# Wide attention tiles: scores shifted and keys summed on the vector engine, one exponential per tile, and the plan that goes with it

## The chip, the core and the metric

The kernel runs on one core of a Trainium2 chip. The metric is the device time of one execution in microseconds (us), median over the runs. Five engines of the core take part: TensorE (PE in the profile, with its weight loads as PEld), VectorE (DVE), ScalarE (ACT), GpSimd (POOL), and SyncE (SP), which issues the DMAs. Each engine works through its own queue in order, and waits on semaphores for the others.

## What is computed

Attention over 4 batches of 8 heads, 576 positions, 64 values per head, is the sum of two parts, one over positions pooled by four and one over a band of seven keys. Its output is the input of two feed-forward layers.

```python
q_d = q.reshape(B, H, Sd, factor, D).mean(axis=3)      # k_d, v_d the same
out_up = np.repeat(sm_attn(q_d, k_d, v_d), factor, axis=2)
mask = np.abs(pos[:, None] - pos[None, :]) < factor
scores = np.where(mask, scale * np.matmul(q, k.transpose(0, 1, 3, 2)), -1e9)
attn = np.exp(scores - np.max(scores, axis=-1, keepdims=True))
attn = attn / (np.sum(attn, axis=-1, keepdims=True) + 1e-09)
x = out_up + np.matmul(attn, v)                        # 2304 tokens x 512
...
xn = x / rms * rms_g
h1 = (silu(xn @ w_gate) * (xn @ w_val)) @ w_out        # 512 -> 1536 -> 512
out = (np.maximum(h1 @ w_in, 0.0) ** 2) @ w_out2       # 512 -> 2048 -> 512
```

## The kernel before

**The two layers.** Every large matrix product is done as three products of float32r parts (high x high, high x low, low x high), so each weight half and each activation exists as a high and a low tile (`xh` and `xl` for the normalised tokens, `hh` and `hl` for the hidden values). The first layer works on nine blocks of 256 tokens (`BLK`) and six slices of 256 hidden columns. A step is `hidden(j, fp)` (lines 920 to 937: 24 matmuls into bank `g`, 24 into bank `v`, then tanh, two multiplications and the split into `hh` and `hl`) and, one step later, `outp(j, fp)` (24 matmuls into the banks `a` or `b`). The string `SEQ` gives the blocks of the first twelve steps, `011100001101`: block 0 once, block 1 three times, and so on. The second layer follows with blocks of 512 tokens.

**The weights** come in as float64 words, and `decode` (line 543) turns each half of 512 columns into float32 high and low parts: a DMA, two passes on ACT, three to four on DVE, an integer addition and a subtraction that POOL or DVE may take (`VP`). For two of the weight tiles, `TAGS` sends an intermediate to a PSUM bank (`a3`, `g1`), and then some of this is done on DVE alone.

**The attention of batch 0** (blocks 0, 1 and a quarter of block 2) is done by PE: `down(b, pr)` (line 614) is the pooled part for a pair of heads, `wide(t)` (line 702) the banded part for 96 tokens and all eight heads, t = 0 to 5, and `wide_post(t)` (line 737) multiplies by v, adds the pooled part, normalises, transposes and writes the columns of `xh` and `xl`. In `wide`, PE writes the scores of four head pairs side by side into two banks (96 tokens by 4 x 104 keys each). DVE takes the maxima (two reductions of 96x416) and scales them; ACT takes eight exponentials of 96x104, each with its own bias and with an accumulator output that gives the sum over keys. Then PE transposes the eight results. The batches 1 to 3 are done without PE, by `local` (line 799) on POOL and DVE, and `post` (line 856).

**What sets the order.** Nothing is issued in program order. The calls are recorded in the order of the string `PLAN` (a = wide, b = wide_post, d = down, w = weights, u = local units, p = post, x = a step of the first layer), and `Plan.order` (line 365) then places every operation on its engine by its own table of costs, going forth and back `ROUNDS` times with some random jitter `JIT`; operations with a choice of engines go to the one that finishes first. `Plan.trace` (line 434) issues them in that order. Where PE would idle before the first block's matmuls, `trace` puts in filler matmuls on the identity (line 466) that write bank `v` and are used by nobody:

```python
fill = fill and not op.ends        # ends: another matmul writes slot v0
if fill and free:
    for _ in range(int((s - free) * FILL / 0.22)):
        self.nc.tensor.matmul(out=out, lhsT=one, rhs=one, start=True, stop=True)
```

All operations are issued from one line (473 before, 472 after the change; fillers 466 and 465), so the profile is read by tile names. `b` followed by a number in the order of instructions is a slice of one of sixteen big SBUF tiles or a PSUM bank `b`; the profile leaves the number out.

Of the kernel before, what the change touches and what calls it, by code (L numbers as in the profile page):

```python
# [48 lines left out]
TAGS = ('dbg- dtg- dbg- dgg- bdd- bdd- bdd- bdd- ttd- ttd- ttd- ttd- add- add- add- add- '  # L49
        'aagg aagg aagt bbtd bbdd bbtd bdt tdt gta gdt gdt btt '  # L50
        '-- -- a3 a3 -- -- -- -- -- -- -- -- -- -- -- -- -- -- -- g1 g1 -- -- -- -- -- -- -- -- -- -- -- -- -- -- --')
SEQ = '011100001101'
PLAN = 'd2 d3 d0 d1 a0 b0 w00 a2 a1 w01 w12 b1 a4 b2 a3 a5 w11 w21 b4 w20 w10 b3 w02 w30 u1 w32 b5 d7 u0 d5 d4 d6 w22 E w31 w41 w40 w50 x x w42 x x d10 x x w52 w51 x x x x x p2 x u2 d11 u3 p3 x d8 x x u5 d9 u4 x x x p4 u6 x x d12 x x x d15 d14 d13 x u7 p5 u8 x u9 x x x x x p6 x x x u10 x x x u11 x x p7 x x u12 u13 x x x x x x x x p8 x x x x x x'
SLOT = [7, 8, 9, 1, 0, 4, 5, 2, 6, 3, 0, 1, 3, 4, 5, 2]
ROUNDS = 38
# [7 lines left out]
JIT = 0.3  # L63
# [413 lines left out]
def attn_moe_kernel(ctx: ExitStack, tc, qs, kw, vw, qt, kt, vt, v4, wg, wv, wo, w2i, w2o, gw, gb,  # L477
# [6 lines left out]
    seq1 = [(int(c), SEQ[:i].count(c)) for i, c in enumerate(SEQ)]  # L484
    seq1 += [(j, fp) for j in range(len(set(SEQ)), len(BLK)) for fp in range(NP1)]
# [57 lines left out]
    def decode(src, n, hi, lo, st, how="--"):  # L543
# [6 lines left out]
        low = lw if how[0] == "-" else bank(how[0], I32)  # L550
        A.activation(low, lw.bitcast(U32), AF.Copy, scale=2.0**-29)
        part = lw if how[1] == "1" else low
        V.scalar_tensor_tensor(out=part, in0=hw, scalar=-0x40000000, in1=low, op0=ALU.bitwise_and,
                               op1=ALU.bitwise_or)
# [5 lines left out]
        if how[1] in "-1":  # L560
            VP.tensor_tensor(out=hw, in0=hw, in1=part, op=ALU.add)
        else:
            V.tensor_tensor(out=low if how[1] == "3" else hw, in0=hw, in1=low, op=ALU.add)
        if how[1] == "3":
            hf = low.bitcast(F32)
        AV.copy(hi[:, cs], hf)
        (V if how[1] == "3" else VP).tensor_tensor(out=lo[:, cs], in0=hf, in1=hi[:, cs].bitcast(F32), op=ALU.subtract)
# [27 lines left out]
    def weights1(fp, m):  # L595
        src = (wg, wv, wo)[m]
        n = fp * 3 + m
        how = TAGS.split()[28 + 2 * n:30 + 2 * n]
        hi, lo = slots(n) if n < 16 else [spare([128, 1024], F32R) for i in range(2)]
        for n in range(2):  # L600
            st = staging() if fp < 5 else tile("stage", "st", [128, 512, 2], I32, 3)
            decode(src[fp], n, hi, lo, st, how[n])
        W1[fp, m] = hi, lo
# [8 lines left out]
    wq, wk, wod = [None] * 4, [None] * 4, [None] * 4  # L612

    def down(b, pr):
# [24 lines left out]
        V.tensor_reduce(out=qs, in_=q[:, 0:S].rearrange("p (s f) -> p s f", f=FAC), axis=AX.X, op=ALU.add)  # L639
# [5 lines left out]
        kf = k[:, 4:4 + S].rearrange("p (s f) -> p f s", f=FAC)  # L645
        if tags[3] == "-":
            V.tensor_reduce(out=ks, in_=k[:, 4:4 + S].rearrange("p (s f) -> p s f", f=FAC), axis=AX.X, op=ALU.add)
        P.memset(vs[:, :, :, 64:65], 4.0)
        V.tensor_reduce(out=vs.rearrange("p c h e -> p (c h) e")[:, :, 0:64], in_=v4s, axis=AX.X, op=ALU.add)
        sps = bank(tags[0])[0:96, 0:432].rearrange("p (c t) -> p c t", c=3)  # L650
        with plan.joint():
            for c in range(3):
                for f in range(1 if tags[3] == "-" else FAC):
                    T.matmul(out=sps[:, c, :], lhsT=qbd[:, c].rearrange("p h t -> p (h t)"),
                             rhs=ks if tags[3] == "-" else kf[:, f], start=(c == 0 and f == 0), stop=(c == 2),
                             skip_group_check=True)
# [45 lines left out]
    def wide(t):  # L702
# [476 lines left out]
```

## Time and profile before

| what | value |
|---|---|
| median of 3 runs | 1001.02 us (1000.61 to 1002.26) |
| the profiled execution: time | 1000.25 us |
| its span (first to last instruction) | 998.0 us |
| PE busy | 980.2 us, 6866 instructions |
| DVE busy | 587.6 us, 985 instructions |
| ACT busy | 417.0 us, 984 instructions |
| POOL busy | 442.3 us, 298 instructions |
| mean granted PE clock | 0.998 |

A float32 matmul appears in the trace as two instructions (two passes). Durations of instructions that follow each other on an engine overlap by some tens of ns, so a start-to-start distance is a little shorter than a duration. Filler matmuls count as busy time of PE.

### The profile page before, as it was taken

How to read it: one execution, taken by the hardware profiler on the slowest of the kernel's cores; microseconds unless marked ns; L12 is line 12 of the kernel's file. 1: busy time of each engine (PE TensorE's matmuls, PEld its weight loads, DVE VectorE, ACT ScalarE, POOL GpSimd, SP SyncE). 2: the span in 40 equal slices, each digit the busy share in tenths (PEclk: the TensorE clock that was granted, in tenths of full speed). 3: DMA queues.
4: the chain of work that ended last, by engine and by line, in shares of the span. 5: the costliest groups of instructions: out<-in, count | busy, mean ns of one | idle time of the engine just before them, and what ended most of it. 6: DMA issues, size and time to landing. Idle time of an engine off the chain costs nothing.

```text
span 998.0 us, 17246 instructions
## 1 busy us (share of the span) xinstructions
PE 980.2 (98%) x6866; PEld 906.4 (91%) x6866; DVE 587.6 (59%) x985; ACT 417.0 (42%) x984; POOL 442.3 (44%) x298
## 2 busy tenths in 40 slices
PE   7998999999999999999999999999999999999998
PEld 7888999999999999999999998888888888888897
DVE  6999899786687857575634568963222322322232
ACT  5787665532435342323244557663222212322232
POOL 2566688867656676676733465863001000100000
PEclk9999999999999999999999999999999999999999
DMA  9954553253262523222011446334000100100010
GB/s 282 262 160 157 175 179 103 73 151 113 85 182 80 171 78 115 93 65 96 28 33 60 132 128 209 104 109 137 1 1 1 54 0 1 43 1 1 1 43 22
DMA packets 38465, 92.93 MB, mean 93 GB/s; under 512 B 4218, under 2 KB 14498, under 8 KB 38386
## 3 DMA queue, kind: packets, MB, share of 16 engines
q1 hardware_dynamic: 38386, 91.84, 29.6%
q8 instruction: 54, 0.88, 0.4%
q14 instruction: 25, 0.20, 0.1%
HBM read 80.62 MB, written 11.21 MB: 92 GB/s over the span
## 4 chain that ended last, share of the span: by engine, by line
PE 89%; DVE 5%; POOL 2%; DMA 2%; issue 1%; ACT 1%; SPq 0%; DVEq 0%; POOLq 0%; ACTq 0%
PE v L473 25%; PE g L473 24%; PE a L473 20%; PE b L473 15%; DVE b L473 2%; PE d L473 2%; DVE st L473 2%; PE t L473 2%; PE v L466 1%; DMA b<-in_qt 1%; DMA st<-in_wg 1%; POOL w L473 0%; POOL st L473 0%; POOL pr L473 0%; POOL b L473 0%
## 5 line engine op out<-in xcount | busy, mean ns | idle before, releaser
L473 PE MATMUL g<-xh,w 128*128 128x256 f32 (+1 forms) x776 | 176.8, 307 | 0.4 <-DVE th L473 0.4
L473 PE MATMUL v<-xh,w 128*128 128x256 f32 (+1 forms) x632 | 147.6, 311 | 0.5 <-DVE hl L473 0.5
L473 DVE SCALAR_TENSOR_TENSOR v<-v,th 128x512 f32<-128x512 f32 (+1 forms) x94 | 63.3, 674 | 128.6 <-ACT th L473 101.3
L473 PEld LDWEIGHTS g<-xh,w 128*128 128x128 f32 x776 | 131.1, 191 | 7.0 <-ACT xh L473 0.6
L473 ACT ACTIVATE th<-g 128x512 f32<-128x512 f32 (+1 forms) x94 | 54.5, 580 | 198.1 <-PE g L473 194.8
L473 POOL TENSOR_TENSOR pr<-v,es 128x896 f32<-128x896 f32 x54 | 99.4, 1939 | 65.7 <-DVE es L473 28.2
L473 PE MATMUL v<-xh,b 128*128 128x256 f32 (+1 forms) x552 | 123.9, 303 | 0.1
L473 POOL TENSOR_TENSOR pr<-k,q 128x896 f32<-128x896 f32 x54 | 115.4, 2158 | 9.6 <-DVE sc L473 7.2
L473 PE MATMUL g<-xl,w 128*128 128x256 f32 (+1 forms) x388 | 118.3, 305 | 0.1
L473 PEld LDWEIGHTS v<-xh,w 128*128 128x128 f32 x632 | 107.7, 191 | 7.1 <-PE g L473 0.7
L473 POOL TENSOR_TENSOR xl<-st,xh 128x1024 fp32r<-128x1024 f32 (+1 forms) x10 | 21.6, 2179 | 184.7 <-ACT xh L473 184.7
L473 PE MATMUL v<-xl,w 128*128 128x256 f32 (+1 forms) x316 | 97.9, 310 | 0.0
L473 PEld LDWEIGHTS v<-xh,b 128*128 128x128 f32 x552 | 93.0, 191 | 4.4 <-PE g L473 0.3
L473 PE MATMUL g<-xh,b 128*128 128x256 f32 (+1 forms) x408 | 94.4, 310 | 0.2 <-DVE th L473 0.2
L473 ACT CAST hh<-v 128x512 fp32r<-128x512 f32 (+1 forms) x94 | 53.5, 569 | 81.6 <-DVE v L473 71.3
L473 PE MATMUL v<-xl,b 128*128 128x256 f32 (+1 forms) x276 | 83.1, 301 | 0.0
L473 DVE SCALAR_TENSOR_TENSOR g<-g,th 128x512 f32<-128x512 f32 (+1 forms) x40 | 25.8, 645 | 95.5 <-ACT th L473 95.4
L473 DVE TENSOR_TENSOR hl<-v,hh 128x512 fp32r<-128x512 f32 (+1 forms) x94 | 62.4, 664 | 26.3 <-ACT hh L473 24.6
L473 PEld LDWEIGHTS g<-xl,w 128*128 128x128 f32 x388 | 74.1, 191 | 3.6 <-DVE xl L473 0.3
L473 POOL TENSOR_TENSOR st<-st 128x512 int32<-128x512 int32 x48 | 55.9, 1166 | 41.5 <-DVE st L473 39.4
L473 PEld LDWEIGHTS g<-xh,b 128*128 128x128 f32 x408 | 69.1, 190 | 4.2 <-issue 0.3
L473 ACT ACTIVATE st<-st 128x512 int32<-128x512 uint32 (+1 forms) x96 | 64.7, 684 | 18.7 <-DVE st L473 11.2
(207 smaller groups left out, 2336.8 us busy)
## 6 DMA issues: line engine op xcount, KB each, us to landing
k<-in_kw SPq DMA_DIRECT2D x12, 640.0 KB
v<-in_vw SPq DMA_DIRECT2D x12, 640.0 KB
st<-in_w2i SPq DMA_DIRECT2D x14, 512.0 KB
st<-in_w2o SPq DMA_DIRECT2D x14, 512.0 KB
y<-vv SPq DMA_DIRECT2D x18, 256.0 KB
out<-xh SPq DMA_DIRECT2D x18, 256.0 KB
st<-y SPq DMA_DIRECT2D x8, 512.0 KB
st<-in_wg SPq DMA_DIRECT2D x7, 512.0 KB
```

What stands on the lines that cost most here:

```text
L466: self.nc.tensor.matmul(out=out, lhsT=one, rhs=one, start=True, stop=True)
L473: getattr(self.hw[on[op]], method)(*args, **kw)
```

## The change

In `wide`, with a fifth letter in the tile's entry of `TAGS` (all six tiles have one now), DVE adds the negated maxima to the scores and writes the shifted scores to SBUF (two instructions of 96x416), ACT takes one exponential over all 96x832 in place, and DVE sums it over the keys (one reduction of 832 to 8). The scaling of the maxima and the eight exponentials with their accumulators go. In `down`, a sixth, fifth or fourth letter sends the pooling sum of v, q or k to PE (`total`, four matmuls with the identity that add up in a bank, and a copy by ACT or DVE); it is used for v of pair 0 and k of pair 3 of batch 0. In `decode` the variants through PSUM go. `PLAN`, `SLOT`, the banks in `TAGS`, `ROUNDS` (38 to 5) and `JIT` (0.3 to 0.05) are others, so the whole order is another; `SEQ` is kept, as the last word of `TAGS`.

```diff
-TAGS = ('dbg- dtg- dbg- dgg- bdd- ...
-        'aagg aagg aagt bbtd bbdd bbtd bdt tdt gta gdt gdt btt '
+TAGS = ('dbg--b dtg--- dbg--- dggt-- bdd--- ...
+        'aaggm aaggm aagtm bbtdm bbddm bbtdm bdt tdt gtd gdt vdt btt '
+        '011100001101')
...
+    def total(parts, tag):
+        n = math.prod(parts.index.shape[1:])
+        p = parts.parts[1] - parts.parts[0]
+        o = bank(tag)[0:p, 0:n]
+        with plan.joint():
+            for f in range(FAC):
+                T.matmul(out=o, lhsT=id_sb[0:p, 0:p], rhs=parts[:, f], start=f == 0, stop=f == FAC - 1)
+        return o
...
+        elif tags[3] != "p":
+            AV.copy(ks, total(kf, tags[3]))
...
+            AV.copy(vo, total(v4s.rearrange("p g d f -> p f g d"), tags[5]).rearrange("p (g d) -> p g d", g=4))
...
         for h in range(2):
             V.tensor_reduce(out=nm[:, 4 * h:4 * h + 4], in_=sp[h], axis=AX.X, op=ALU.max, negate=True)
-        V.tensor_scalar(out=nm, in0=nm, scalar1=SCALE, scalar2=None, op0=ALU.mult)
-        for h in range(2):
-            for r in range(4):
-                i = 4 * h + r
-                A.activation(p[:, h, r], sp[h][:, r], AF.Exp, bias=nm[:, i:i + 1], scale=SCALE,
-                             accum_out=sm_[:, i:i + 1])
+            for h in range(2):
+                V.tensor_tensor(out=p[:, h], in0=sp[h], in1=nm[:, 4 * h:4 * h + 4].unsqueeze(2).to_broadcast([WT, 4, WK]),
+                                op=ALU.add)
+            pf = p.rearrange("p h r k -> p (h r) k")
+            A.activation(pf, pf, AF.Exp, scale=SCALE)
+            V.tensor_reduce(out=sm_, in_=pf, axis=AX.X, op=ALU.add)
```

The places of the order on which the prediction rests follow, first those before, then those of the change.

DVE's queue at the first wide tile. `b_89` is a slice that holds maxima and sums, `a` the bank of the scores, `b_244` the exponentials of the tile. Before:

```order
L473 TENSOR_REDUCE b_89<-a 96x4 x2
L473 TENSOR_SCALAR b_89<-b_89 96x8
L473 TENSOR_SCALAR rc<-g 72x4
L473 TENSOR_REDUCE vs<-w_203 72x4x64
L473 RECIPROCAL rc<-rc 72x4
L473 TENSOR_REDUCE nm<-d 96x3
```

After:

```order
L472 TENSOR_REDUCE b_89<-a 96x4 x2
L472 TENSOR_TENSOR b_244<-a,b_89 96x416 x2
L472 SCALAR_TENSOR_TENSOR st<-st 128x512
L472 TENSOR_SCALAR rc<-g 72x4
L472 TENSOR_REDUCE vs<-w_190 72x4x64
L472 RECIPROCAL rc<-rc 72x4
L472 TENSOR_REDUCE nm<-d 96x3
L472 TENSOR_TENSOR b_313<-g,rc 72x256
L472 TENSOR_REDUCE b_89<-b_244 96x8
```

The scaling is gone from behind the maxima; two additions stand there, and a sum over 832 elements stands six instructions further down. The same holds for all six tiles.

PE's queue ahead of the first matmul of block 0 (`v_1104`, after the change `v_791`). `v_134` are fillers, `t` and `d` are transposes and the pooled part in banks. Before:

```order
L473 MATMUL b_995<-b8_412,b6_200 96x64 x8
L466 MATMUL v_134<-id_101 128x128 x19
L473 MATMUL t_1059<-id_101,b9_470 128x96 x4
L473 MATMUL d_1067<-id_101,pe_1025 72x96 x3
L466 MATMUL v_134<-id_101 128x128 x3
L473 MATMUL b_1078<-b11_351,qbd_95 96x144 x3
...
L473 MATMUL v_1104<-xh_554,w16_796 128x256
```

After:

```order
L472 MATMUL v_721<-b8_349,b5_417 96x64 x8
L472 MATMUL d_753<-id_101,b9_502 128x96 x4
L472 MATMUL t_759<-id_101,b3_675 104x96 x4
L472 MATMUL t_776<-id_101,b1_461 104x96 x4
L472 MATMUL d_783<-id_101,b3_675 104x96 x4
L472 MATMUL v_791<-xh_563,w18_639 128x256
```

One wide_post now multiplies into bank `v` (`v_721`), which ends the fillers; before, they run up to the last matmuls ahead of block 0. In all there are 151 filler matmuls before and 64 after.

PE's queue at the first matmul of block 1 (`g_1239`, after the change `g_1119`; `xh_1010` and `xh_770` are block 1). Before:

```order
L473 MATMUL g_1176<-xh_554,w15_429 128x256
L473 MATMUL t_1213<-id_101,b9_470 128x96 x4
L473 MATMUL d_1229<-id_101,pe_1169 72x96 x3
L473 MATMUL g_1239<-xh_1010,w14_408 128x256
```

After:

```order
L472 MATMUL d_1085<-id_101,pe_1067 72x96 x3
L472 MATMUL t_1095<-id_101,b9_502 128x96 x4
L472 MATMUL d_1108<-id_101,pe_1067 72x96 x3
L472 MATMUL g_1119<-xh_770,w14_362 128x256
```

In both, the transposes of the last wide tile (`t_1213`, `t_1095`) stand right ahead of it, and 48 matmuls of 128x256, all of block 0, are ahead of that. Before, the second half of them comes directly in front; after the change they are all done earlier, with small matmuls in between.

DVE's queue at the last columns of block 1 (`xl_1018`, after the change `xl_774`). Before:

```order
L473 SCALAR_TENSOR_TENSOR b9_470<-t_1093,b15_89,b7_337 96x512
L473 SCALAR_TENSOR_TENSOR b12_442<-b12_442 128x512
L473 RECIPROCAL rc_1173<-rc_1173 72x4
L473 TENSOR_SCALAR b13_262<-b13_262 128x512
L473 TENSOR_TENSOR pt_1224<-d_1122,rc_1173 72x256
L473 SCALAR_TENSOR_TENSOR th_1220<-th_1220,g_1176 128x512
L473 TENSOR_TENSOR xl_1018<-t_1213,xh_1010 128x4x32
```

After:

```order
L472 SCALAR_TENSOR_TENSOR b9_502<-t_999,b15_89,b7_269 96x512
L472 TENSOR_TENSOR es_1059<-es_1059,ssum_1069 128x2x2x7
L472 TENSOR_REDUCE vs_1032<-b14_442 72x4x64
L472 TENSOR_SCALAR b13_227<-b13_227 128x512
L472 SCALAR_TENSOR_TENSOR th_958<-th_958,g_888 128x512
L472 TENSOR_TENSOR xl_774<-t_1095,xh_770 128x4x32
```

Ahead of this point DVE has, of decode, 20 bitwise combinations (SCALAR_TENSOR_TENSOR of `st` or `b`) and 35 TENSOR_SCALAR before, 19 and 38 after; four more decode instructions that read bank `a` only before; and of the local attention four reductions of 896 elements before (two `sc<-pr`, two `xa<-pr`), two after (`sc<-pr`).

## Rows read from the trace of the kernel before

**Rows 1.** The page: span, and busy time (share, instructions) of each engine.

```profile
span 998.0 us, 17246 instructions
...
PE 980.2 (98%) x6866; PEld 906.4 (91%) x6866; DVE 587.6 (59%) x985; ACT 417.0 (42%) x984; POOL 442.3 (44%) x298
```

**Rows 2.** Busy time of each engine by stretches; the first column is the stretch.

```profile
core 0: us, PE busy (x) PEld busy (x) DVE busy (x) ACT busy (x) POOL busy (x), PEclk, DMA share, GB/s
3.79:104.73 100.94, 92.68 (x841) 84.77 (x842) 89.92 (x171) 75.28 (x229) 55.23 (x47) 0.98 0.70 215
104.73:205.00 100.27, 98.90 (x843) 98.18 (x844) 89.33 (x133) 56.38 (x119) 77.95 (x55) 1.00 0.45 135
205.00:990.00 785.00, 784.58 (x5167) 720.42 (x5166) 405.85 (x675) 282.86 (x634) 308.82 (x191) 1.00 0.23 72
```

**Rows 3.** Timeline of PE: start, duration, what, and idle time before it.

```profile
71.11 0.90 PE L473 MATMUL b<-b,qbd 128*96 128x144 f32 x6
...
72.29 1.04 PE L473 MATMUL d<-b,b 72*96 72x128 f32 x8
...
91.94 1.54 PE L473 MATMUL b<-b,qbd 128*96 128x144 f32 x6 [1.15 <-ACT st L473]
...
93.75 1.91 PE L473 MATMUL t<-b,b 72*96 72x128 f32 x8
...
104.73 0.35 PE L473 MATMUL g<-xh,w 128*128 128x256 f32 x1 [0.44 <-DVE th L473]
```

**Rows 4.** Timeline of DVE: a tile's maxima and scaling, the last maxima, block 1's last columns.

```profile
17.09 1.07 DVE L473 TENSOR_REDUCE b<-a 96x4 f32<-96x416 f32 x2
18.20 0.17 DVE L473 TENSOR_SCALAR b<-b 96x8 f32<-96x8 f32 x1
...
65.05 0.57 DVE L473 TENSOR_REDUCE b<-b 96x4 f32<-96x416 f32 x1
...
104.88 0.29 DVE L473 TENSOR_TENSOR xl<-t,xh 128x128 fp32r<-128x128 f32 x1 [0.29 <-ACT xr L473]
```

**Rows 5.** Groups of DVE by form, 0 to 150 us: busy us, mean ns, idle before.

```profile
L473 DVE TENSOR_REDUCE w<-w 128x144 f32<-128x576 f32 x8 | 5.9, 744 | 3.8 <-DMA w<-in_qt 3.7
...
L473 DVE TENSOR_REDUCE vs<-w 72x256 f32<-72x1024 f32 x4 | 4.8, 1209 | 0.0
...
L473 DVE TENSOR_REDUCE sc<-pr 128x14 f32<-128x896 f32 x4 | 4.3, 1069 | 0.0
...
L473 DVE TENSOR_TENSOR b<-g,b 96x512 f32<-96x512 f32 x3 | 2.0, 680 | 0.0
...
L473 DVE CUSTOM_DVE_ANT_0 a<-st,a 128x1024 uint16<-128x1024 uint16 x1 | 0.7, 680 | 0.0
```

**Rows 6.** ACT: groups of a tile's exponentials, a longer activation by form (0 to 110 us).

```profile
L473 ACT ACTIVATE b<-a,b 96x104 f32<-96x104 f32 x24 | 8.0, 344 | 1.8 <-DVE b L473 1.8
...
L473 ACT ACTIVATE b<-b 128x512 f32<-128x512 f32 x9 | 6.2, 692 | 0.7 <-DVE b L473 0.7
...
L473 ACT ACTIVATION_READ_ACCUMULATOR b<-a,b 96x1 f32 x24 | 4.9, 203 | 0.0
```

**Rows 7.** Timeline of ACT: the sixth tile's last exponential.

```profile
79.82 0.34 ACT L473 ACTIVATE b<-b,b 96x104 f32<-96x104 f32 x1
```

**Rows 8.** Waits of DVE, 3.7 to 105.2 us: total, times, longest.

```profile
DVE b L473 <- POOL b L473: 2.7, 2, 1.4
...
DVE b L473 <- ACT b L473: 1.1, 1, 1.1
```

**Rows 9.** Groups of POOL by form, 0 to 200 us: a decode's addition and its subtraction.

```profile
L473 POOL TENSOR_TENSOR st<-st 128x512 int32<-128x512 int32 x20 | 22.9, 1145 | 10.7 <-DVE st L473 10.4 <-DVE b L473 0.4
...
L473 POOL TENSOR_TENSOR w<-b,w 128x512 fp32r<-128x512 f32 x9 | 12.9, 1437 | 4.7 <-ACT w L473 4.7
```

**Rows 10.** Groups of PE by form, 0 to 150 us: the fillers.

```profile
L466 PE MATMUL v<-id 128*128 128x128 f32 x302 | 40.9, 285 | 0.0
```

More of the change, by code (lines that the diff above doesn't have):

```diff
@@ L62 @@
 FILL = 0.8
-JIT = 0.3
+JIT = 0.05
 SEED = 1
@@ L483, in attn_moe_kernel @@
     blk2 = [(n, min(512, NT - n)) for n in range(0, NT, 512)]
-    seq1 = [(int(c), SEQ[:i].count(c)) for i, c in enumerate(SEQ)]
-    seq1 += [(j, fp) for j in range(len(set(SEQ)), len(BLK)) for fp in range(NP1)]
+    seq = TAGS.split()[-1]
+    seq1 = [(int(c), seq[:i].count(c)) for i, c in enumerate(seq)]
+    seq1 += [(j, fp) for j in range(len(set(seq)), len(BLK)) for fp in range(NP1)]
     seq2 = [(j, f) for j in range(len(blk2)) for f in range(2 * NP2)]
@@ L541, in attn_moe_kernel, with decode @@
     late = []
-    def decode(src, n, hi, lo, st, how="--"):
+    def decode(src, n, hi, lo, st):
         DQ.dma_start(out=st.rearrange("p n w -> p (n w)"),
@@ L549, in decode @@
         hf = hw.bitcast(F32)
[L550 to L554, printed above, removed]
+        A.activation(lw, lw.bitcast(U32), AF.Copy, scale=2.0**-29)
+        V.scalar_tensor_tensor(out=lw, in0=hw, scalar=-0x40000000, in1=lw, op0=ALU.bitwise_and, op1=ALU.bitwise_or)
         plan.either(A=lambda e: e.activation(hf, hf, AF.Abs),
@@ L559, in decode @@
                         op1=ALU.logical_shift_left)
[L560 to L565, printed above, removed]
+        VP.tensor_tensor(out=hw, in0=hw, in1=lw, op=ALU.add)
         AV.copy(hi[:, cs], hf)
-        (V if how[1] == "3" else VP).tensor_tensor(out=lo[:, cs], in0=hf, in1=hi[:, cs].bitcast(F32), op=ALU.subtract)
+        VP.tensor_tensor(out=lo[:, cs], in0=hf, in1=hi[:, cs].bitcast(F32), op=ALU.subtract)
     stages = [0, 0]
@@ L597, in weights1 @@
         n = fp * 3 + m
-        how = TAGS.split()[28 + 2 * n:30 + 2 * n]
         hi, lo = slots(n) if n < 16 else [spare([128, 1024], F32R) for i in range(2)]
@@ L601, in weights1 @@
             st = staging() if fp < 5 else tile("stage", "st", [128, 512, 2], I32, 3)
-            decode(src[fp], n, hi, lo, st, how[n])
+            decode(src[fp], n, hi, lo, st)
         W1[fp, m] = hi, lo
@@ L638, in down @@
         pt = tile("dn", "pt", [72, 2, 2, 3, 48])
-        V.tensor_reduce(out=qs, in_=q[:, 0:S].rearrange("p (s f) -> p s f", f=FAC), axis=AX.X, op=ALU.add)
+        qf = q[:, 0:S].rearrange("p (s f) -> p f s", f=FAC)
+        kf = k[:, 4:4 + S].rearrange("p (s f) -> p f s", f=FAC)
+        if tags[4] == "-":
+            V.tensor_reduce(out=qs, in_=qf.rearrange("p f s -> p s f"), axis=AX.X, op=ALU.add)
+        else:
+            qs = total(qf, tags[4])
         for h in range(2):
@@ L652, in down @@
             for c in range(3):
-                for f in range(1 if tags[3] == "-" else FAC):
+                for f in range(FAC if tags[3] == "p" else 1):
                     T.matmul(out=sps[:, c, :], lhsT=qbd[:, c].rearrange("p h t -> p (h t)"),
-                             rhs=ks if tags[3] == "-" else kf[:, f], start=(c == 0 and f == 0), stop=(c == 2),
+                             rhs=kf[:, f] if tags[3] == "p" else ks, start=(c == 0 and f == 0), stop=(c == 2),
                              skip_group_check=True)
@@ L720, in wide @@
             V.tensor_reduce(out=nm[:, 4 * h:4 * h + 4], in_=sp[h], axis=AX.X, op=ALU.max, negate=True)
-        V.tensor_scalar(out=nm, in0=nm, scalar1=SCALE, scalar2=None, op0=ALU.mult)
-        for h in range(2):
-            for r in range(4):
-                i = 4 * h + r
-                A.activation(p[:, h, r], sp[h][:, r], AF.Exp, bias=nm[:, i:i + 1], scale=SCALE,
-                             accum_out=sm_[:, i:i + 1])
+        if tags[4] == "-":
+            V.tensor_scalar(out=nm, in0=nm, scalar1=SCALE, scalar2=None, op0=ALU.mult)
+            for h in range(2):
+                for r in range(4):
+                    i = 4 * h + r
+                    A.activation(p[:, h, r], sp[h][:, r], AF.Exp, bias=nm[:, i:i + 1], scale=SCALE,
+                                 accum_out=sm_[:, i:i + 1])
+        else:
+            for h in range(2):
+                V.tensor_tensor(out=p[:, h], in0=sp[h], in1=nm[:, 4 * h:4 * h + 4].unsqueeze(2).to_broadcast([WT, 4, WK]),
[3 more added lines that the diff above has]
+            V.tensor_reduce(out=sm_, in_=pf, axis=AX.X, op=ALU.add)
         V.tensor_scalar(out=sm_, in0=sm_, scalar1=1e-9, scalar2=None, op0=ALU.add)
```

18 lines of the change are left out of this document (9 added, 9 removed).

## The prediction

> **What bounds the kernel now.** I read the page first, for who is busy. PE is, with 98% of the span, DVE with 59% [rows 1]. A share over the whole span hides that the program has two regimes, so the second view is the busy time by stretches [rows 2]. From 205 to 990 us PE is busy 784.58 of 785.00 us: the feed-forward layers run without a gap, and nothing beside PE counts. From 104.73 to 205 us it is busy 98.90 of 100.27 us. Before 104.73 us DVE is busy 89.92 of 100.94 us, ACT 75.28 and POOL 55.23. PE shows 92.68 us there too, but much of that is filler: 302 passes of 285 ns, which overlap [rows 10], are used by nobody.
>
> What ends the first regime is in the timeline of PE: at 104.73 us the first matmul of block 1 starts [rows 3], and from then on the PE is full. It can start when the last columns of block 1 are written, which DVE does at 104.88 us, some 0.15 us behind the first pass, for the low part [rows 4]. I call this point **the gate**. Behind it PE has the same work in both versions: counting the order up to the gate, the forms and numbers of PE's instructions agree but for the fillers, the eight matmuls of the pooling sums that the change adds ahead of it, and three small ones each way. So the time moves by what the gate moves, plus any new stall behind it. The fillers themselves are no gain: they fill time in which PE waits anyway.
>
> **The sum.** DVE's queue up to the gate holds all six wide tiles in both versions, so I price what the change puts into and takes out of it.
>
> - Added: twelve additions of 96x416 from PSUM. The trace has no such form; the nearest row multiplies a bank of 96x512 by a broadcast factor in 680 ns [rows 5], so 680 x 416/512 = 553 ns, in all 6.6 us. Six sums of 96x832: a reduction of 896 elements takes 1069 ns [rows 5], so 993 ns, in all 6.0 us. Together 12.6 us. Bounds: start to start some 0.08 us less each, so 11.2, and up to 13 if a longer tile costs a little more.
> - Removed: six scalings at 0.17 us [rows 4], 1.0 us; the pooling sums of k and v for one pair each, 744 and 1209 ns [rows 5], 1.95 us; four decode instructions through bank a, each like the one of 680 ns [rows 5], 2.7 us. Two reductions of 896 elements for the local attention stand behind the gate now, 2.1 us. The rest of decode is as much as before (one combination less, three scalar passes more), taken at nothing, give or take 0.5 us.
>
> That is 12.6 - 1.0 - 1.95 - 2.7 - 2.1 = **+4.9 us** of DVE work ahead of the gate.
>
> DVE was idle for 100.94 - 89.92 = 11.0 us there [rows 2]. More work in an in-order queue covers some waits. DVE waited 2.7 us for POOL's powers and 1.1 us for ACT [rows 8]; ACT has less to do now. Eight exponentials at 344 ns and eight accumulator reads at 203 ns [rows 6] go for one instruction of 832 elements, by the row of 692 ns for 512 elements about 1.1 us. I let half of these 3.8 us go: **-2.0 us**, between 0 and the whole 11.0.
>
> The clock. The granted clock is 0.98 over the first stretch [rows 2], with one low place: at 91.94 us, behind an idle time of 1.15 us, six passes take 1.54 us that took 0.90 at 71.11, and at 93.75 eight take 1.91 where a like group took 1.04 at 72.29 [rows 3]. That place cost 0.6 + 0.9 = 1.5 us, at the lower of the two levels (1.2 GHz). The change leaves 64 of 151 fillers and ends them far ahead of the gate, when one product is written into bank v; between the first 48 matmuls of block 0 and the gate PE has only small work. I expect block 1 to begin at the low level and lose this once: **+1.5 us**, between 0 and 3. The Trainium skill says the same of idle gaps (TensorE: Matmul & The Clock Gate, Why this matters for your kernels): matmul bursts are to follow each other without gaps, or the array falls back to its lower clock. The one low place of the trace agrees with it.
>
> Taken at nothing: the eight added pooling matmuls and their copies (in the first 15 us, where PE and ACT wait for DMAs and DVE); the two decode halves whose addition and subtraction go from DVE to POOL, 2 x (1145 + 1437) = 5.2 us [rows 9], since POOL is busy 55.23 of 100.94 us [rows 2]; and the two reductions put off, since DVE is idle 100.27 - 89.33 = 10.9 us from 104.73 to 205 [rows 2]. If that cover is gone, the second rival holds. Wide scores also leave their banks earlier, when DVE has added and not when ACT has finished; this only helps PE, which waits.
>
> 4.9 - 2.0 + 1.5 = +4.4 us on the profiled execution's 1000.25 us (span 998.0), 1004.7 us. The median of the runs is 0.77 us above that execution, so **1005.4 us**.
>
> A rule of the skill stands against this reading. By Perfetto Trace Analysis, Identifying the Most-Contended Engine, the engine with the highest occupancy is the one to optimize; over the span that is PE, and by it 12.6 us on an engine at 59% [rows 1] would cost nothing, some 1001 us. The stretches [rows 2] contradict it for the first 105 us; the same page, under Optimization Strategy, grants that the most contended engine may change between regimes.
>
> **The rivals.**
>
> *Faster: the chain of the tiles, not DVE's queue, sets the gate.* The sixth tile's maxima end at 65.6 us [rows 4], but its last exponential comes at 79.82 us [rows 7], since ACT takes the eight one by one between other work. In the change, two additions (1.1 us) and one exponential (1.1 us) follow the maxima, so the tile could be ready some 12 us sooner. But DVE has to get through its queue: with no idle time at all it needs 89.9 + 4.9 = 94.8 us where the stretch took 100.9, so the gate comes at most 6.1 us sooner, 995 us; halfway 998 us. It decides for "faster" if DVE's idle time ahead of the gate falls from 11.0 us to under 4. For it: the idle time is all waits for others, and the whole order is another. Against it: DVE's queue is mostly work of decode and down, placed between the tiles.
>
> *Slower still: what is put off does not fit behind the gate.* The two reductions (2.1 us) and POOL's 5.2 us come due before block 2 is needed at about 205 us; POOL is busy 77.95 and DVE 89.33 of 100.27 us there [rows 2]. If none of it fits, 1005.4 + 7.3 = 1012.7 us. It decides once PE idles by several us between the gate and the end of block 1's steps, where it idled 1.4 us.
>
> *No change.* DVE's waits take up the 4.9 us whole and the clock stays high at the gate, 1001 us.
>
> That the change does not do what it says is excluded: all six tiles have the fifth letter, and the order shows twelve additions of 96x416 and six exponentials of 96x832. Only the maxima were on DVE already, so that part changes nothing.
>
> **How the numbers follow.** No change is within 0.2%, 999 to 1003 us; less than this a measurement can't tell. The forecast (gate late by 2 to 9 us, 1003 to 1009) has 0.44, slower still 0.13, no change 0.15, faster 0.28: the order is wholly rearranged, and a few us of waits decide. So slower by over 0.2% has 0.57. The range leaves under one in ten on each side: from the lower bound of the faster rival, 995, to the second rival's time, 1012.5.
>
> **What would show it.** Right: the first matmul of block 1 starts 2 to 7 us after 104.73 us; DVE is busy over 90% of the time until then, with twelve additions near 0.55 us and six sums near 1.0 us; the clock reads below 1.00 in the stretch before it, and behind it PE idles as little as before. The step on the waits is wrong if DVE's idle time up to the gate is under 6 us; the step on the clock, if block 1's first passes run at full pace. The whole is wrong if the gate comes before 103 us, or if PE is fuller ahead of it with block 0's or other useful steps than the order lets me see.

## The result, and the profile after

The changed kernel takes 1012.33 us (median of 4 runs, 1011.6 to 1013.95), the kernel before, beside it on the same chip, 1001.64 us (4 runs, 1000.61 to 1005.26): ratio 1.0102, 95% interval [1.0073, 1.0132]. The change makes it slower by 10.7 us; forecast were 4.4. The profiled execution took 1013.95 us, its span is 1011.9 us.

The page, which answers to [rows 1]: PE is busy for about as long as before, DVE 6.8 us longer, ACT 11.5 us less.

```profile
span 1011.9 us, 16829 instructions
...
PE 982.2 (97%) x6708; PEld 904.1 (89%) x6708; DVE 594.4 (59%) x991; ACT 405.5 (40%) x896; POOL 445.9 (44%) x302
```

Busy time by stretches, which answers to [rows 2]. The stretch up to the gate is shown whole and in three pieces.

```profile
core 0: us, PE busy (x) PEld busy (x) DVE busy (x) ACT busy (x) POOL busy (x), PEclk, DMA share, GB/s
3.79:25.00 21.21, 19.61 (x132) 16.25 (x133) 11.26 (x21) 8.58 (x26) 0.20 (x2) 1.00 0.99 289
25.00:75.00 50.00, 41.51 (x387) 34.84 (x385) 48.97 (x90) 30.62 (x59) 27.89 (x23) 0.92 0.55 166
75.00:115.71 40.71, 29.70 (x167) 26.97 (x165) 32.76 (x69) 26.87 (x58) 28.18 (x24) 0.58 0.49 151
3.79:115.71 111.92, 90.82 (x681) 78.06 (x681) 92.99 (x178) 66.07 (x142) 56.28 (x49) 0.81 0.61 184
115.71:205.00 89.29, 89.29 (x734) 89.29 (x735) 80.05 (x116) 48.88 (x100) 70.07 (x49) 0.95 0.44 141
```

The same pieces of the kernel before:

```profile
3.79:25.00 21.21, 19.52 (x174) 18.40 (x175) 16.34 (x28) 11.46 (x41) 4.84 (x5) 1.00 0.98 305
25.00:75.00 50.00, 47.86 (x456) 41.95 (x455) 46.73 (x96) 40.55 (x134) 30.60 (x24) 1.00 0.71 211
75.00:104.73 29.73, 25.30 (x217) 24.42 (x216) 26.86 (x49) 23.27 (x56) 19.79 (x19) 0.94 0.48 158
```

The gate, block 1's first matmul, has moved from 104.73 to 115.71 us, by 11.0 us. DVE's work ahead of it has grown by 92.99 - 89.92 = 3.1 us, its idle time from 11.02 to 18.93 us, by 7.9. By pieces (length less DVE busy) that idle time was 4.87, 3.27 and 2.87 us before and is 9.95, 1.03 and 7.95 us now: between 25 and 75 us DVE hardly pauses any more, and 5.1 us came in on either side.

The timeline of PE shows what stands in the first piece, a late group of the tiles, and the gate, which answers to [rows 3]:

```profile
5.26 1.73 PE L472 MATMUL d<-w,b 128*96 128x144 f32 x6 [5.26 <-DVE w L472]
7.12 3.84 PE L472 MATMUL b<-w,id 72*72 72x256 f32 x8
10.79 2.23 PE L472 MATMUL t<-w,id 128*128 128x144 f32 x8
...
14.68 1.50 PE L472 MATMUL d<-w,qbd 128*96 128x144 f32 x6
...
17.99 0.90 PE L472 MATMUL d<-w,b 128*96 128x144 f32 x6
...
81.46 1.97 PE L472 MATMUL d<-b,b 72*96 72x128 f32 x8
...
115.71 0.55 PE L472 MATMUL g<-xh,w 128*128 128x256 f32 x1 [0.97 <-ACT pt L472]
...
124.80 0.55 PE L472 MATMUL v<-xh,w 128*128 128x256 f32 x2
125.18 0.28 PE L472 MATMUL v<-xl,w 128*128 128x256 f32 x1
```

The second and third rows are the pooling sums that the change moved to PE. They take from 7.12 to 12.84 us and stand ahead of the scores of the next pair of heads (14.68). PE is at half pace here: the group at 5.26 takes 1.73 us, the same form at 17.99 takes 0.90, although the clock column reads 1.00 for this piece. The kernel before starts at half pace too, but 18 fillers stand where the pooling sums stand now, and full pace is there by 11.05 us:

```profile
5.49 1.72 PE L473 MATMUL d<-w,b 128*96 128x144 f32 x6 [5.49 <-DVE w L473]
7.00 3.71 PE L466 MATMUL v<-id 128*128 128x128 f32 x18
...
11.05 0.90 PE L473 MATMUL d<-w,qbd 128*96 128x144 f32 x6
```

Behind the gate the first pass takes 0.55 us where it took 0.35 [rows 3]; only at 125.2 us are passes back to 0.28.

The timeline of DVE, which answers to [rows 4]: the two longest waits, and block 1's last columns.

```profile
16.21 0.60 DVE L472 TENSOR_REDUCE nm<-d 96x3 f32<-96x432 f32 x1 [4.99 <-PE d L472]
...
83.53 0.69 DVE L472 TENSOR_TENSOR d<-b,d 96x512 f32<-96x512 f32 x1 [3.75 <-PE d L472]
...
115.49 0.28 DVE L472 TENSOR_TENSOR xl<-t,xh 128x128 fp32r<-128x128 f32 x1
```

Both waits are for PE: the first for the scores behind the pooling sums, the second for the group at 81.46, which stands behind block 0's passes at half pace and takes 1.97 us where a like group took 1.04 [rows 3]. The forms of DVE up to the gate (busy us, mean ns, idle before), which answer to [rows 5]:

```profile
L472 DVE TENSOR_REDUCE b<-b 96x8 f32<-96x832 f32 x6 | 6.0, 1005 | 0.0
...
L472 DVE TENSOR_TENSOR b<-a,b 96x416 f32<-96x416 f32 x6 | 3.2, 576 | 0.0
L472 DVE TENSOR_TENSOR b<-b,b 96x416 f32<-96x416 f32 x6 | 3.2, 573 | 0.0
```

### The profile page after: what moved, and what is told of

It reads as the page before. It is cut to its first block, busy times and chain, and to the rows that moved or that the text cites. A ratio compares the mean times of both kernels' runs of the same rounds, so it can differ in the third digit from the quotient of the medians.

```text
span 1011.9 us, 16829 instructions
## 1 busy us (share of the span) xinstructions
PE 982.2 (97%) x6708; PEld 904.1 (89%) x6708; DVE 594.4 (59%) x991; ACT 405.5 (40%) x896; POOL 445.9 (44%) x302
## 4 chain that ended last, share of the span: by engine, by line
PE 90%; DVE 5%; POOL 2%; issue 2%; DMA 1%; ACT 1%; SPq 0%; POOLq 0%
PE g L472 25%; PE v L472 25%; PE a L472 20%; PE b L472 16%; DVE b L472 3%; PE d L472 2%; PE t L472 2%; POOL w L472 1%; POOL b L472 1%; DVE st L472 1%; DVE xl L472 0%; DMA w<-in_v 0%; ACT xh L472 0%; POOL st L472 0%; DMA od<-pt 0%
## 5 line engine op out<-in xcount | busy, mean ns | idle before, releaser
L472 PE MATMUL g<-xh,w 128*128 128x256 f32 (+1 forms) x776 | 180.4, 311 | 1.0 <-ACT pt L472 1.0
L472 PE MATMUL v<-xh,w 128*128 128x256 f32 (+1 forms) x632 | 150.8, 316 | 0.0
L472 PEld LDWEIGHTS g<-xh,w 128*128 128x128 f32 x776 | 134.1, 195 | 7.7 <-ACT pt L472 1.3
L472 PEld LDWEIGHTS v<-xh,w 128*128 128x128 f32 x632 | 110.0, 195 | 6.4
```

Of the source, the lines that this page charges most:

```text
L472: getattr(self.hw[on[op]], method)(*args, **kw)
```

## The experiments

Twelve kernels, each beside runs of the kernel before on its own chip. All keep the order of the kernel they start from: the plan is made as there, and in `trace` an operation's calls are replaced at its place (`swap`, an empty list for none), or fillers are added or left out. So a difference comes from the edit and from the waits that it shifts, not from a new plan. The table sums them up: the gate in the profile, what the span is beyond it, DVE's busy and idle time from 3.79 us to the gate, and the ratio of the runs to before.

| kernel | gate | span - gate | DVE busy | DVE idle | ratio [95%] |
|---|---|---|---|---|---|
| before | 104.73 | 893.3 | 89.92 | 11.02 | 1 |
| after | 115.71 | 896.2 | 92.99 | 18.93 | 1.0102 [1.0073, 1.0132] |
| e1 before, fillers end early | 109.98 | 894.3 | 89.76 | 16.43 | 1.0028 [1.0010, 1.0046] |
| e2 after, fillers up to the gate | 121.03 | 892.8 | 98.01 | 19.23 | 1.0119 [1.0086, 1.0152] |
| e3 before, maxima three times | 114.18 | 894.7 | 102.91 | 7.48 | 1.0084 [1.0057, 1.0111] |
| e4 after, short sums | 112.77 | 895.6 | 88.69 | 20.29 | 1.0054 [1.0038, 1.0070] |
| f5 after, pooling sums on DVE | 113.44 | 893.8 | 96.68 | 12.97 | 1.0056 [1.0029, 1.0083] |
| f6 after, old exponentials | 117.99 | 895.9 | 83.74 | 30.46 | 1.0165 [1.0135, 1.0194] |
| f7 before, wide part | 118.56 | 895.1 | 102.08 | 12.69 | 1.0106 [1.0073, 1.0138] |
| f8 after, f5 and f6 together | 119.11 | 893.9 | 86.74 | 28.58 | 1.0130 [1.0107, 1.0152] |
| g1 before, wide part, sums earlier | 115.84 | 894.0 | 101.21 | 10.84 | 1.0112 [1.0065, 1.0158] |
| g2 after, fillers in unused columns | 128.53 | 893.8 | 96.40 | 28.34 | 1.0200 [1.0159, 1.0240] |
| g3 before, two decodes on POOL | 114.11 | 894.9 | 86.97 | 23.35 | 1.0048 [1.0028, 1.0069] |
| h1 f5 with fillers in a free bank | 112.74 | 893.8 | 96.56 | 12.39 | 1.0065 [1.0051, 1.0079] |

The third column holds within 3.4 us over all fourteen, while the gate ranges over 24 us: whatever is edited ahead of the gate, the rest of the kernel follows it as it is. The profiles are single executions and scatter by some us against the medians, so the ratios decide where the two disagree (as for e1 and g3). A difference between two of the kernels carries both intervals, some 3 to 4 us.

**Is it the clock? (e1, e2)** e1 ends the fillers of the kernel before at 60 us of the plan, as the change does:

```diff
-                    if fill and free:
+                    if fill and free and s < 60.0:
```

> The kernel before in its own order, but with no fillers placed after 60 us of the plan, where the changed kernel places its last ones. Theory A (the loss of the changed kernel is the clock: without fillers PE falls to the low level ahead of the gate, its small matmuls of the tile chain take twice as long, and block 1 starts at half pace): the granted clock falls to about 0.5 to 0.7 between 65 and 105 us, the gate moves from 104.7 to 109 or later, and the time is 5 to 10 us longer, 1006 to 1011. Theory B (the loss is DVE's longer queue, the clock costs little): the gate stays within 2 us and the time within 3 us, 1001 to 1004.

Measured: 1.0028, 2.8 us. DVE's work is the same, but it idles 5.4 us more, and the gate comes at 109.98 us, at full pace. The low clock of the stretch ahead (0.82 against 0.98 in that stretch) delays what DVE waits for; the runs put that at 2.8 us, about a quarter of the change's loss.

e2 gives the changed kernel 93 more fillers from 65 us to the gate, each in the bank that the next group of matmuls writes:

```diff
+    for _ in range(more):      # 93 in all, ahead of 12 groups
+        self.nc.tensor.matmul(out=fb[:, 0:128], lhsT=one, rhs=one, start=True, stop=True)
```

> The changed kernel in its own order, with 93 more fillers between 65 us and the first matmul of block 1, each written into the bank that the next group of matmuls overwrites. Theory A: the clock stays at 1.0 up to the gate, the gate moves from 115.7 to 107 to 110, block 1 starts at full pace, and the time falls by 6 to 9 us, to 1003 to 1006. Theory B: the gate stays after 112, only the low stretch behind it goes, and the time falls by 2 to 4 us, to 1008 to 1010.

Measured: 1.0119, not better than the change. Block 1 begins at full pace and the span beyond the gate falls to 892.8 us, but the gate comes at 121.03. The wait of 3.75 us for PE is gone; two other things took its place. A filler that writes the next group's bank waits until that bank is free, and then stands in front of the group, as PE's timeline shows (line 472 is the filler):

```profile
73.66 3.35 PE L472 MATMUL t<-id 128*128 128x128 f32 x14 [2.70 <-ACT b L479]
...
88.73 4.77 PE L472 MATMUL g<-id 128*128 128x128 f32 x26 [3.07 <-DVE b L479]
```

And DVE's idle time is only 0.3 us more than after the change, but the same 178 instructions keep it busy 5.0 us longer. Part of it is three TENSOR_SCALAR that took 0.99 us after the change and take 2.96 here, while POOL runs two subtractions (84.79 to 87.70 us; the last section comes back to this). First the change, then e2:

```profile
84.47 0.99 DVE L472 TENSOR_SCALAR b<-b 128x512 f32<-128x512 f32 x3
85.04 2.96 DVE L479 TENSOR_SCALAR b<-b 128x512 f32<-128x512 f32 x3
```

The gain behind the gate, 896.2 - 892.8 = 3.4 us, is about what the low level costs there; the gate's place is not explained by the clock.

**Is it DVE's queue? (e3, e4)** e3 issues each of the twelve maxima of the kernel before three times, e4 cuts the change's six sums from 104 keys per head to one:

```diff
+    if on[op] == "V" and calls[0][2].get("negate") and calls[0][2]["out"].shape == (96, 4):
+        calls = calls * 3
...
+    if method == "tensor_reduce" and kw["out"].shape == (96, 8):
+        kw = dict(kw, in_=kw["in_"][:, :, 0:1])
```

> The kernel before in its own order, each of the twelve maxima issued three times: 24 x 0.53 = 12.7 us of added DVE work, as much as the additions and sums of the change, nothing taken away, fillers as they are. Theory B: the gate moves by 8 to 13 us and the time is 1009 to 1014. Theory A: DVE's waits take up a good part, the gate moves by at most 5 us, 1002 to 1006.

> The changed kernel in its own order, the six sums over 832 elements cut to one key per head (the denominators are left out but for one term): 6 x 0.9 = 5.4 us less DVE work ahead of the gate. Theory B: the gate moves from 115.7 to 110 to 111 and the time falls by 4 to 6 us, to 1006 to 1008. Theory A: PE's and ACT's waits stay, and the time falls by less than 2 us, 1010 to 1013.

Measured: e3 has 13.0 us more DVE work, 3.5 us less idle time, the gate 9.45 us later and ratio 1.0084; e4 4.3 us less work, the gate 2.9 us earlier and ratio 1.0054, 4.8 us below the change. So work on DVE moves the gate, at some 0.7 us per us, in both orders. The maxima and the sums also stand in the chain of their own tile, so these two runs do not tell DVE's queue from that chain.

**The parts of the change undone (f5, f6, f8).** f5 makes the two pooling sums with one DVE reduction each again:

```diff
             AV.copy(ks, total(kf, tags[3]))
+            plan.ops[-2].swap = []
+            plan.ops[-1].swap = [("V", "tensor_reduce", (), dict(out=ks, in_=kf..., axis=AX.X, op=ALU.add))]
```

> The changed kernel, its order kept, but the two pooling sums that it makes with matmuls and a copy (k of one pair, v of another, in the opening 15 us) are made by one reduction each on the vector engine again. Theory Q (the loss is the longer vector queue and its waits; the pooling matmuls, 3.84 + 2.23 us of PE in front of the second pair's scores, cause the 4.99 us wait of nm<-d at 11 us): that wait falls under 1.5 us, the queue grows by 1.95 us, the gate comes 2 to 4 us before 115.71 us, the time 2 to 4 us below the changed kernel's 1012.3 (ratio to before near 1.007). Theory C (the low TensorE clock is the loss): the time stays within 1 us of 1012.3.

Measured: 1.0056, 4.6 us below the change, although DVE is busy 3.7 us longer. PE's timeline from 5 us on:

```profile
5.36 1.72 PE L473 MATMUL d<-w,b 128*96 128x144 f32 x6 [5.36 <-DVE w L473]
8.19 1.39 PE L473 MATMUL b<-id,pe 96*72 96x96 f32 x6 [1.11 <-ACT pe L473]
9.37 1.12 PE L465 MATMUL v<-id 128*128 128x128 f32 x4
10.31 1.73 PE L473 MATMUL d<-w,qbd 128*96 128x144 f32 x6
```

The first piece of its stretches, columns as above:

```profile
3.79:25.00 21.21, 18.54 (x125) 16.30 (x126) 14.47 (x25) 9.60 (x27) 0.20 (x2) 1.00 0.99 281
```

The second pair's scores come at 10.31 instead of 14.68 us, and DVE idles 6.7 us there instead of 9.95. Of the 4.7 us of span, 2.3 are the gate and 2.4 lie behind it, where the half pace ends at 116 us instead of 125. So theory Q was right on the gate, and low on the time by what lies behind it. The 6.7 us are still 1.9 more than before: the 18 fillers of the kernel before are not in this order, and PE stays at half pace up to some 17 us (1.73 us at 10.31 for the form that takes 0.90 at 11.05 before).

f6 undoes the wide part in the change's order:

```diff
                 V.tensor_tensor(out=p[:, h], in0=sp[h], in1=nm[...]..., op=ALU.add)
+                plan.ops[-1].swap = []
+            plan.ops[-1].swap = [("V", "tensor_scalar", ...SCALE...)] + eight ("A", "activation", ..., accum_out=...)
...
             A.activation(pf, pf, AF.Exp, scale=SCALE)
+            plan.ops[-1].swap = []
             V.tensor_reduce(out=sm_, in_=pf, axis=AX.X, op=ALU.add)
+            plan.ops[-1].swap = []
```

> The changed kernel, its order kept, but the wide part undone in all six tiles: no additions and no sums on the vector engine (12.6 us less), eight exponentials with their own sums per tile on ScalarE at the place of the second addition, the scaling of the maxima back (1.0 us). Theory Q: the gate comes 6 to 9 us earlier, 107 to 110 us, time 1003 to 1006 (ratio to before 1.002 to 1.004). Theory O (what is lost is lost by the other order of the work and by its early end of the fillers, whatever the queue holds): under 3 us earlier, ratio 1.007 or more. Theory C: the pace behind the gate stays low and the time stays above 1009.

Measured: 1.0165, slower than the change by 6 us; no theory expected that. DVE's queue is 9.3 us shorter, and its idle time 11.5 us longer. The piece of its stretches from 25 to 75 us:

```profile
25.00:75.00 50.00, 44.78 (x394) 37.11 (x394) 33.82 (x75) 36.76 (x130) 25.34 (x23) 0.90 0.49 146
```

DVE is busy 33.82 of 50 us there, after the change 48.97. The eight take 2.6 us of ACT in one piece where one takes 0.91; PE waits for them before the third tile's scores (0.82 and 0.37 us), and DVE, with less to do, waits for PE. But not all of this is the exponentials' length. In the second to fifth tile the eight stand in ACT's queue where the one stood; in the first and the sixth the edit puts them ahead of other work, in the first of a copy for `down` (`pt`) behind which the one stood. ACT, PE and DVE in f6:

```profile
21.82 0.33 ACT L473 ACTIVATE b<-a,b 96x104 f32<-96x104 f32 x1
...
24.41 0.40 ACT L473 COPY pt<-g 72x288 f32<-72x288 f32 x1
...
24.96 1.22 PE L473 MATMUL g<-vs,pt 72*72 72x65 f32 x16 [2.32 <-ACT pt L473]
...
26.22 0.16 DVE L473 TENSOR_SCALAR rc<-g 72x4 f32<-72x4 f32 x1 [3.57 <-PE g L473]
```

ACT after the change:

```profile
22.85 0.39 ACT L472 COPY pt<-g 72x288 f32<-72x288 f32 x1
...
23.93 0.91 ACT L472 ACTIVATE b<-b 96x832 f32<-96x832 f32 x1
```

DVE's longest wait between the opening and 75 us, 3.57 us up to 26.22, is thus for `down` behind the eight, not for a tile. So in this order a DVE queue shorter by 9.3 us is no gain if ACT's work is longer; how much of the 6 us is due to the place that the eight were given, no run tells.

f8 undoes both:

> The changed kernel, its order kept, with both undone: pooling sums on the vector engine and the eight exponentials on ScalarE. What is left of the change is its order, its fillers and its decode. Theory Q: the two gains add up to 8 to 12 us, the gate at 104 to 108 us and the time within 3 us of before (ratio 0.998 to 1.003). Theory O: the gate stays beyond 109 us and the ratio at 1.005 or more. Theory C: the pace behind the gate stays low and costs 3 to 5 us, ratio 1.003 to 1.005.

Measured: 1.0130. Against f6 the pooling sums give back 3.5 us (4.6 in f5), at the edge of what the intervals tell; the profile has the gate 1.1 us later than f6 and 2.0 us less behind it. What is left, 13 us above before with the old exponentials and pooling sums, belongs to the rest of the change (order, fillers, decode) and to the place of the eight. That the order, laid for the wide form, is the main part is likely and not shown.

**The wide part alone (f7, g1).** In the kernel before, the two additions and the one exponential stand where the first of the eight exponentials stood; the sum stands in front of its first use (f7) or where the eighth stood (g1):

```diff
+                if i == 0:
+                    plan.ops[-1].swap = [two ("V", "tensor_tensor", ..., op=ALU.add)] + [("A", "activation", (pf, pf, AF.Exp), ...)]
+                if i == 7:
+                    plan.ops[-1].swap = [("V", "tensor_reduce", (), dict(out=sm_, in_=pf, axis=AX.X, op=ALU.add))]
```

> The kernel before, its order, fillers and pooling sums kept, but all six tiles have the wide part: two additions and one sum on the vector engine, one exponential of 832 elements on ScalarE at the place of the first of the eight. Theory Q: 11.6 us more vector work ahead of the gate; at the 0.75 us of gate per us of work that the tripled maxima showed, the gate moves by 7 to 10 us from 104.73, and block 1's first passes run at full pace: 1008 to 1012, ratio 1.007 to 1.010. If ScalarE's shorter work shortens the chain (the rival of the prediction): gate moves by under 4 us, ratio under 1.004. Theory C: fillers go on as before, so the time stays within 2 us of before.

> The kernel before with its order, fillers, decode and pooling sums, and the wide part in all six tiles as in the run before, but each sum over keys stands on the vector engine where the eighth exponential stood in the order, not in front of its first use. Theory Q (the vector queue ahead of the gate): 11.6 us more work there, so as the run before: gate 8 to 14 us later than 104.73 us, ratio 1.007 to 1.012, pace behind the gate full. If the lateness of the sums made the run before so slow: ratio under 1.005.

Measured: 1.0106 and 1.0112, gates at 118.56 and 115.84 us, full pace behind them. In both, the sixth tile's second half is transposed (and in g1 summed) ahead of its exponential, since the order has that half's exponentials first, so that tile's output is another; number and size of the instructions are those of the wide part. It costs as much alone as the whole change does: 11.3 us more DVE work in g1 makes 11.1 us of gate, with DVE's idle time as before (10.84 and 11.02 us).

**The clock again (g2, h1), and decode (g3).** g2's fillers stand behind a group of matmuls and write columns of its bank that nobody uses:

```diff
+    for _ in range(more):
+        self.nc.tensor.matmul(out=banks[at0].get()[:, lo:hi], lhsT=one, rhs=one[:, 0:hi - lo], start=True, stop=True)
```

> The changed kernel, its order kept, with 81 more filler passes between 66 us and the gate that wait for nothing: they stand behind a group of matmuls and write the columns of a bank that no one uses. Theory C' (the low TensorE clock is one part of the loss: block 0's passes at half pace keep the vector engine waiting 3.7 us at 80 us, and block 1's first 9 us run at half pace): both go, the gate comes 2 to 5 us before 115.71 us at full pace, and the time falls by 4 to 8 us to 1004 to 1008. If the clock costs only what stands behind the gate: 3 to 4 us. Theory Q alone: no change of over 1.5 us.

Measured: 1.0200, far from every expectation. DVE's waits, total, times and longest, say why (line 486 is the filler):

```profile
DVE nm L481 <- PE b L486: 9.0, 2, 6.8
...
DVE b L481 <- PE b L486: 5.5, 1, 5.5
```

The reader of a bank waited for the last matmul that wrote it, and that was now a filler. The run tells nothing on the clock.

h1 starts from f5 and writes 64 fillers to bank `a`, which nothing uses between the third tile's scores and the gate:

```diff
+    for _ in range(MORE.get(op.n, 0)):
+        self.nc.tensor.matmul(out=banks[158].get()[:, 0:128], lhsT=one, rhs=one, start=True, stop=True)
```

> The changed kernel with its two pooling sums on the vector engine, as in the run of that name (ratio 1.0056, gate at 113.44 us in its profile, first passes at half pace), and with 64 filler passes between 65 us and the gate that wait for nothing: they write bank a, which nothing uses there, and stand in front of the matmuls ahead of which TensorE idled in that run. Theory C' (the low clock is one part of the loss): the clock stays at 0.95 or more up to the gate, block 1 begins at full pace, which saves 3 to 4 us behind the gate, and the gate comes up to 3 us earlier: ratio to before 0.999 to 1.003. If the fillers only stand in front of the tiles' own matmuls: gate later than 114 us, ratio 1.005 or more. If the clock is not to be had with so few: ratio 1.004 to 1.006.

Measured: 1.0065 against f5's 1.0056, no difference. Nothing waited for these fillers, and the clock is better but not whole, as two pieces of its stretches show:

```profile
75.00:85.00 10.00, 6.24 (x54) 5.94 (x53) 7.14 (x12) 4.94 (x11) 9.30 (x7) 0.92 0.36 111
85.00:95.00 10.00, 10.00 (x56) 10.00 (x55) 8.55 (x15) 7.73 (x17) 6.02 (x5) 0.57 0.52 162
```

DVE's wait for PE at 77 us fell from 2.34 us in f5 to 0.64, and a wait for ACT of 2.21 us came behind it. So much of a higher clock as these fillers bring does not help this order; what a clock of 1.00 throughout would bring was not reached.

g3 moves two halves of a decode in the kernel before from bank `a` and DVE to SBUF and POOL, as the change does:

```diff
             V.tensor_tensor(out=low if how[1] == "3" else hw, in0=hw, in1=low, op=ALU.add)
+            if three:
+                plan.ops[-1].swap = [("P", "tensor_tensor", (), dict(out=hw, in0=hw, in1=lw, op=ALU.add))]
```

> The kernel before, its order kept, with one part of the change alone: the two decode halves of weight matrix 1 that go through bank a and the vector engine (two additions, two subtractions, 2.7 us) go through SBUF and POOL instead (5.2 us there). Theory Q: the queue falls by 2.7 us, the gate comes 1 to 2.5 us earlier, the time 1 to 2.5 us below before (ratio 0.9975 to 0.999). If POOL is in the way there: same or up to 2 us slower.

Measured: 1.0048, slower. One of the two halves is loaded anew before its last two steps read it, so that part of a weight is another. DVE has 2.95 us less to do and idles 12.3 us more. The other half keeps its stage until POOL is done with it, and the next load into that stage is issued later. SP's queue in the kernel before:

```profile
60.64 0.33 SPq L473 DMA_DIRECT2D st<-in_wv  x1
```

The same load in g3:

```profile
71.92 0.33 SPq L476 DMA_DIRECT2D st<-in_wv  x1
```

ACT's first pass on a stage behind it, in g3:

```profile
76.02 0.66 ACT L476 ACTIVATE st<-st 128x512 int32<-128x512 uint32 x1 [5.80 <-DMA st<-in_wv]
```

In the order of before, the way through bank `a` frees the stage early, and that was worth more than the DVE time. DVE's longest wait, 4.13 us at 76.71 us, is for this pass; the rest of the 12.3 us is spread over other waits, of which POOL's are the next largest (4.0 us, 2.7 before). In the change's order the loads are placed anew, and ACT waits for no load of a stage `st` up to the gate, so this is no term of its loss.

No run beats the kernel before; the best form of the change that still does all its work, f5, is 5.6 us slower.

## Why the prediction came out as it did

It forecast slower by 4.4 us through a gate that moves; it became slower by 10.7 us through a gate that moved. Sign and path were right. The make-up of the move was not: the sum had it from DVE's added work, less some waits, and most of it is added waits. That the time lies inside the range, by 0.2 us, is luck: the upper bound is the time of the rival *slower still*, which did not happen, and the forecast's own band (gate late by 2 to 9 us, 1003 to 1009 us) was passed.

- **"The time moves by what the gate moves, plus any new stall behind it."** Right, and the surest result: span less gate is 892.8 to 896.2 us in fourteen kernels. Behind the gate PE is busy 89.29 of 89.29 us up to 205 us, so the rival *slower still* is out: what was put off fitted. What the gate waited for last before was DVE's `th`, which its row names [rows 3], and not the last columns; `th` stands right ahead of them in DVE's queue, so the reading is the same. (After the change the row names ACT's `pt`, which ends 0.13 us behind `th`.)
- **DVE's work, +4.9 us.** Measured +3.1 of busy time. The sum adds whole durations, while busy time counts the overlap of neighbours once; with the prediction's own lower bound for the additions and sums, start to start (11.2 us), it gives 3.5. Additions and sums were priced well (575 and 1005 ns, estimated 553 and 993), the wide exponential takes 0.90 us (estimated 1.1). That more work moves the gate is shown alone by e3, f7 and g1 in the order before and by e4 in the order after. In the change's own order, e4 (4.8 us) and f5 (4.6 us) give back most of the loss if they add up, which no run tests.
- **The waits, -2.0 us.** This is the term that failed: they grew by 7.9 us. "More work in an in-order queue covers some waits" held between 25 and 75 us (3.27 to 1.03 us), and in e3 (3.5 us less with 13 us more work). It failed at both ends.
  - In the opening, 5.1 us, the step is "the eight added pooling matmuls and their copies (in the first 15 us, where PE and ACT wait for DMAs and DVE)", taken at nothing. PE did have time, but its queue is in order: 5.7 us of matmuls, at half pace, went in front of the second pair's scores, and DVE, with nothing else ready, waited 4.99 us for them. f5 shows their price: 4.6 us of time, 2.3 of it at the gate, more than the 1.95 us of DVE work that they saved. It takes back 3.2 of the 5.1 us; the other 1.9 go with PE's half pace up to 17 us, which no run tests.
  - From 75 us on, 5.1 us more. The longest wait, 3.75 us at 83.53, is for PE, which works there at a granted clock of 0.58 on average. In the order before, a clock that is lost in this way cost 2.8 us (e1). In the change's order, fillers took this wait away and others took its place (e2, h1). A rival that no run tests is POOL, which the prediction took at nothing: in the profile's chain from 75 us to the gate its instructions have 22.0, 16.2 and 8.3% (`w`, `b`, `st`), where before `w` and `st` had 5.0 and 3.9%. One link of that chain is doubtful: a POOL instruction at 111.76 us that is put down to a DMA starts right behind DVE's 96x1 (111.54 for 0.14 us), which may be what it waited for. How the 5.1 us split between clock, loads, POOL and order stays open.
- **The clock at the gate, +1.5 us, between 0 and 3.** Block 1 did begin at the low level, and kept it for 9.5 us: span less gate is 2.9 us more than before, although PE now has none of the 1.4 us of idle time behind the gate; against e2, at full pace, it is 3.4. Right in kind, mis-sized: the row used was a place with 1.15 us of idle time; here PE had been busy for only 4.15 of the last 10 us (105 to 115) before block 1 came. Two readings of the clock were wrong as well. The low place at 91.94 is not the only one before the gate, since the opening runs at half pace up to some 11 us. And the fillers are a gain: without the late ones the kernel before is 2.8 us slower (e1). Nor does idle time alone tell: before the group at 79.69 PE idled 1.63 us, longer than at 91.94, and it ran at full pace.

```profile
79.69 1.08 PE L473 MATMUL d<-b,b 72*96 72x128 f32 x8 [1.63 <-DVE b L473]
```

- **The rival "faster: the chain of the tiles".** In the change's order, taking the short exponential away costs 6 us although DVE has 9.3 us less to do (f6); some of that may be the place of the eight. So its mechanism, which the prediction doubted, has support and a size that is not known. Its own test, DVE idle under 4 us, was not met (18.93), since the idle time sits at the ends and not at the tiles.
- **By its own signs:** the gate should come 2 to 7 us late (it came 11.0 late) and DVE be busy over 90% until then (83%); the clock fell ahead of the gate (0.98 to 0.81), and the sizes of the new instructions were right.

Put together, the profiled spans differ by 13.9 us: 3.1 of DVE work, 7.9 of DVE waits, 2.9 of clock behind the gate. The executions that were profiled lie 1.4 us below the median before and 1.6 above it after, which is the step from 10.7 to 13.7.

## What to carry to other kernels

Find the point from which the bound engine never pauses again, and read every edit by how it moves that point; the difference between span and that point shows at once whether a run is understood. An instruction put on an idle engine is not free if the next thing that others wait for stands behind it in the same queue: ask who waits for its successor. And an order that a planner laid for one form of the work is part of that form: the wide part cost 11 us in one order, and undoing it in the other cost 6 more, so a part that is undone in place is priced in that order only, with the place that the edit gives it.

## What was not expected of the hardware

One form of DVE instruction that takes 0.68 us elsewhere took 2.36 us beside POOL. In the timeline of DVE after the change:

```profile
70.42 2.36 DVE L472 SCALAR_TENSOR_TENSOR b<-b 128x512 int32<-128x512 int32 x1
...
79.10 0.68 DVE L472 SCALAR_TENSOR_TENSOR b<-b 128x512 int32<-128x512 int32 x1
```

And in that of POOL:

```profile
69.69 1.29 POOL L472 TENSOR_TENSOR w<-st,w 128x512 fp32r<-128x512 f32 x1
70.94 1.28 POOL L472 TENSOR_TENSOR w<-b,w 128x512 fp32r<-128x512 f32 x1
```

The first ends 0.56 us after POOL's second subtraction (72.22), as if it had only then begun. The Trainium skill (SBUF — State Buffer, SBUF: two separate sides) says that of a DVE instruction with two SBUF inputs and a GpSimd instruction that reads SBUF, the one that starts first holds the shared ports for its whole length, and the other waits. These rows agree, and here POOL held them twice in a row. So DVE's busy time holds some waiting for POOL: e2 is busy 5.0 us longer on the same instructions, and a queue priced by mean durations has such waiting in it.
